# Aligned load buffers, a later place for flags and slot gates, and a new split of a gather over three engines

## The chip, the cores and the metric

The kernel runs on one core of a Trainium2 chip. The metric is the device time of one execution in microseconds (us): the median of several runs, and the span of one profiled execution, which is the time from its first to its last instruction in the profile.

## The reference

The reference first runs a gated recurrence over each of 4 sequences of 5056 steps with 256 channels, then sends every one of the 20,224 resulting rows to one of 8 experts. Each expert keeps at most the 80 rows with the highest gate weight; all other output rows are zero.

```python
sig = 1.0 / (1.0 + np.exp(-f_logit))
f = lower_bound + (1.0 - lower_bound) * sig
i = 1.0 - f
for t in range(S):                        # 4 sequences, 5056 steps, 256 channels
    h = f[:, t] * h + i[:, t] * x[:, t]
    y[:, t] = h
...
logits = y @ w_gate                       # 20224 rows, 8 experts
expert_idx = np.argmax(logits, axis=1)
gate_w = softmax(logits)[rows, expert_idx]
for e in range(8):
    tok_idx = rows of expert e, the 80 with the largest gate_w
    h = np.maximum(y[tok_idx] @ w1[e], 0.0)             # 256 -> 1024
    out[tok_idx] = gate_w[tok_idx, None] * (h @ w2[e])  # 1024 -> 256
```

All data are float32.

## The kernel before

The kernel has three stages on one core. The order of all instructions is written out by hand: within an engine the program order is the order of execution, and an instruction that waits holds up everything behind it on its engine.

**Loads and recurrence.** The work is cut into 40 units (10 groups of 512 steps by 4 sequences; the last group has 448). A unit loads a block of `f_logit` and a block of `x`, 512 KB each, through SyncE's DMA queue (SP) into the buffers `f_t` and `x_t` of the pool `ld`, four of each. Each partition gets four pieces of 1 KB per block. ScalarE (ACT) makes the sigmoid, GpSimd (POOL) multiplies it with `x`, TensorE (PE) transposes both into the channel layout, ACT and VectorE (DVE) finish the gate and run the scan, and the result stays in `h_all`, a buffer of all 20,224 columns. PE also computes the gate logits of each unit. From the ninth unit on SP also issues a clear of a 256 KB piece of the output for each unit, a copy from a zeroed DRAM buffer; `clear_rest` issues what is left in pieces of 1 MB after the last unit, behind the first six weight halves.

**Selection.** The largest gate weights of each expert are ranked, and the selected token numbers are put into `trow` (8 experts by 80 slots) on DVE, line 577; ACT copies slot gates and token numbers to `flat`, line 578. The function `settle` then does two things. `slots_down` transposes `flat` on PE and makes `gsl` (the gate weight of each slot, which `finish` uses) and `goal` (the output row of each slot, which `scatter` uses). After that DVE computes four flags per partition in `doubts`; they say whether the fast selection could be wrong. PE adds the flags up in `total`, line 687, and DVE turns them into `doubt` after expert 1. Only if `doubt` is above zero does a second, slower branch run.

**Experts.** For each expert e:

- `gather(e)` copies the 80 selected columns of `h_all` into `xe`. Three engines share the 80: each first loads its token numbers from `trow` into registers (line 618) and then copies column by column (line 622). DVE has 28 columns, ACT 28, POOL 24.
- `scaled(e)` on DVE multiplies `xe` into `xt`, in two instructions (line 629).
- `hidden(e)` on PE, 32 matmul passes (line 640), and `relu(e)` on ACT.
- `result(e)` on PE, 16 passes (line 655), and `finish(e)` on DVE, which scales by `gsl`.
- `scatter(e)` on POOL, an indirect DMA of 80 rows into the output.

Weights arrive in halves of 512 KB in the pool `wring`, seven buffers, issued by `more(1)` on SP as buffers come free. `wring` begins where `ld` began once the first stage has closed its pools. `busy(pool, m, tag)` issues m matmuls on PE whose result isn't used; it stands between stages, where PE would otherwise be without work.

The order around the change is `gather(0)`, `scaled(0)`, `settle()`, `busy(psl, 24, "rivals")`, `gather(1)`, `scaled(1)`, `hidden(0)`, `relu(0)`, `total`, `gather(2)`, `result(0)`, `scaled(2)`, `finish(0)`, `hidden(1)`, `relu(1)`; then a loop over e from 1 with `gather(e+2)`, `hidden(e+1)`, `relu(e+1)`, `result(e)`, `scaled(e+2)`, `finish(e)`, `scatter(e-1)`.

The pool `consts` holds the small tables, `trow`, `gsl`, `goal` and others; the `ld` pool follows it. In the built program the first load buffer begins at byte 25,568 of each partition, which is 480 past a multiple of 512, and since all load and weight buffers are 4 KB long and adjacent, each of them does. `h_all` is allocated from the other end of the memory.

Of the kernel before, what the change touches and what calls it, by code (L numbers as in the profile page):

```python
# [9 lines left out]
F32 = mybir.dt.float32  # L10
# [7 lines left out]
P = 128  # L18
# [5 lines left out]
def kernel(  # L24
# [11 lines left out]
    nc = tc.nc  # L36
# [10 lines left out]
    K = (capacity + TOP - 1) // TOP * TOP  # L47
# [22 lines left out]
    consts = ctx.enter_context(tc.tile_pool(name="consts", bufs=1))  # L70
# [31 lines left out]
    ones = consts.tile([P, 1], F32, name="ones")  # L102
# [25 lines left out]
    gsl = consts.tile([K, E], F32, name="gsl")  # L128
    goal = consts.tile([K, E], I32, name="goal")
    doubt = consts.tile([1, 1], I32, name="doubt")  # L130


    hpool = tc.alloc_tile_pool(name="hpool", bufs=1, side="right")
# [30 lines left out]
    def busy(pool, m, tag):  # L164
        warm = pool.tile([P, P], F32, name="warm", tag=tag)
        for _ in range(m):
            nc.tensor.matmul(warm, ident, ident, start=True, stop=True)  # L167
# [319 lines left out]
    def slots_down(flat, sp):  # L487

        nc.tensor.transpose(sp, flat, ident[:2 * E, :2 * E])
        nc.vector.tensor_copy(gsl, sp[:, ds(E, E)])  # L490
        far = consts.tile([K, E], F32, name="far", tag="far")
        nc.vector.tensor_scalar(out=far, in0=gsl, scalar1=0.0, scalar2=AWAY,
                                op0=ALU.is_le, op1=ALU.mult)
        nc.vector.tensor_tensor(goal, sp[:, :E], far, ALU.add)


    doubts = consts.tile([P, 6], F32, name="doubts")
    psl = ctx.enter_context(tc.tile_pool(name="psl", bufs=1, space=PSUM))
    with tc.tile_pool(name="sel", bufs=1) as sel:
# [15 lines left out]
        rivals = psl.tile([P, M + 3], F32, name="rivals", tag="rivals")  # L515
        sums_p = rivals[:, M:]
        rivals = rivals[:, :M]
        nc.tensor.matmul(rivals, mates, spread.rearrange("p c k -> p (c k)"),
                         start=True, stop=True)
# [51 lines left out]
        kept = psl.tile([P, K + 2 * E], F32, name="kept", tag="kept")  # L571
# [8 lines left out]
    def settle():  # L580


        low = consts.tile([P, DEEP], F32, name="low")
        d = doubts
        slots_down(flat, kept[:K, ds(K, 2 * E)])
        nc.vector.tensor_scalar(out=low, in0=taken, scalar1=-2.0, scalar2=2.0,
                                op0=ALU.mult, op1=ALU.add)
        nc.vector.tensor_tensor(low, low, vals, ALU.add)
        nc.vector.tensor_reduce(d[:, 4:5], low, AX.X, ALU.min)
        nc.vector.tensor_reduce(d[:, 5:6], tops[:, :, TOP - 1], AX.X, ALU.max)  # L590
        nc.vector.tensor_copy(d[:, 0:1], taken[:, DEEP - 1:])
        nc.vector.tensor_tensor(d[:, 1:2], d[:, 5:6], d[:, 4:5], ALU.is_ge)
        nc.vector.scalar_tensor_tensor(out=d[:, 2:3], in0=vals[:, ds(TOP - 1, 1)],
                                       scalar=vals[:, ds(TOP, 1)], in1=taken[:, ds(TOP, 1)],
                                       op0=ALU.is_le, op1=ALU.mult)
        nc.vector.tensor_scalar(d[:, 3:4], off[:, 2:3], float(capacity), off[:, 1:2],
                                ALU.min, ALU.not_equal)

    ways = [(mybir.EngineType.DVE, nc.vector.tensor_copy, 28),
            (mybir.EngineType.Activation, nc.scalar.copy, 28),  # L600
            (mybir.EngineType.Pool, nc.gpsimd.tensor_copy, K - 56)]
    ways = [w for w in ways if w[2] > 0]

    def experts(again):
        with tc.tile_pool(name="xp", bufs=2) as xp, \
             tc.tile_pool(name="mp", bufs=2) as mp, \
             tc.tile_pool(name="psh", bufs=4, space=PSUM) as psh, \
             tc.tile_pool(name="psy", bufs=2, space=PSUM) as psy:
            w = {} if again else w_sb
            late = list(order if again else order[3:])  # L610
            X, XT, HID, Y = {}, {}, {}, {}


            def gather(e):
                X[e] = xp.tile([P, DC, K], F32, name="xe", tag="xe")
                k = 0
                for engine, copy, n in ways:
                    _, at_tok = nc.values_load_multi_w_load_instructions(
                        trow[ds(e, 1), ds(k, n)], engines=(engine,), min_val=0, max_val=N - 1,
                        skip_runtime_bounds_check_because="token numbers come from iota")  # L620
                    for j, v in enumerate(at_tok):
                        copy(X[e][:, :, ds(k + j, 1)], h_all[:, :, ds(v, 1)])  # L622
                    k += n

            def scaled(e):
                XT[e] = mp.tile([P, DC, K], F32, name="xt", tag="xt")
                x_e = X.pop(e)
                for o in range(DC):
                    nc.vector.tensor_scalar_mul(XT[e][:, o], x_e[:, o], omlb[:, ds(o, 1)])  # L629

            def hidden(e):
                HID[e] = mp.tile([P, FC, K], F32, name="hid", tag="hid")
                xt = XT.pop(e)
                halves = w.pop((1, e))
                ps = []
                for i in range(2):
                    h_ps = psh.tile([P, CH, K], F32, name="h_ps", tag="h_ps")
                    for c in range(CH):
                        for o in range(DC):
                            nc.tensor.matmul(h_ps[:, c], halves[i][:, o, ds(c * P, P)], xt[:, o],  # L640
                                             start=o == 0, stop=o == DC - 1,
                                             skip_group_check=True)
                    ps.append(h_ps)
                return ps

            def relu(e, ps):
                for i in range(2):
                    nc.scalar.activation(HID[e][:, ds(i * CH, CH)], ps[i], ACT.Relu)  # L648

            def result(e):  # L650
                y_ps = psy.tile([K, D], F32, name="y_ps", tag="y_ps")
                halves = w.pop((2, e))
                hid = HID.pop(e)
                for c in range(FC):
                    nc.tensor.matmul(y_ps, hid[:, c], halves[c // CH][:, c % CH],  # L655
                                     start=c == 0, stop=c == FC - 1)
                return y_ps

            def finish(e, y_ps):
                Y[e] = mp.tile([K, D], F32, name="y", tag="y", bufs=3)  # L660
                nc.vector.tensor_scalar_mul(Y[e], y_ps, gsl[:, ds(e, 1)])  # L661

            def scatter(e):
                nc.gpsimd.indirect_dma_start(  # L664
                    out=out, out_offset=bass.IndirectOffsetOnAxis(ap=goal[:, ds(e, 1)], axis=0),
                    in_=Y.pop(e), in_offset=None, bounds_check=N - 1, oob_is_err=False)

            def more(m):
                for key in late[:m]:
                    w[key] = weights(*key)  # L670
                del late[:m]

            if again:
                more(3)
            gather(0)
            scaled(0)
            if not again:
                settle()
                busy(psl, 24, "rivals")
            gather(1)  # L680
            scaled(1)
            ps = hidden(0)
            relu(0, ps)
            more(1)
            if not again:
                total = psl.tile([1, 4], F32, name="total", tag="kept")
                nc.tensor.matmul(total, ones, doubts[:, :4], start=True, stop=True)
            gather(2)
            y_ps = result(0)
            more(1)  # L690
            scaled(2)
            finish(0, y_ps)
            ps = hidden(1)
            relu(1, ps)
            more(1)
            for e in range(1, E):
                if e + 2 < E:
                    gather(e + 2)
                if e + 1 < E:
                    ps = hidden(e + 1)  # L700
                    relu(e + 1, ps)
                    more(1)
                y_ps = result(e)
                more(1)
                if e + 2 < E:
                    scaled(e + 2)
                finish(e, y_ps)
                scatter(e - 1)
                if e == 1 and not again:
                    found = consts.tile([1, 1], F32, name="found")  # L710
                    nc.vector.tensor_reduce(found, total, AX.X, ALU.add)
                    nc.vector.tensor_copy(doubt, found)
            scatter(E - 1)

    experts(False)


# [83 lines left out]
```

## Time and profile before

| | |
|---|---|
| median of 3 runs | 256.51 us (255.76 to 257.93) |
| the profiled execution's own time | 258.45 us |
| its span in the profile | 256.3 us |
| busy PE, DVE, ACT, POOL | 213.3, 166.1, 138.2, 135.3 us |
| moved by DMA | 81.11 MB, mean 316 GB/s |
| mean granted clock of PE | 0.949 |

The page of the profile cuts the span into 40 equal columns of 6.4 us and gives for each column the busy share of each engine in tenths, the granted PE clock in tenths of full speed, the share of the 16 DMA engines and the rate. In lists of instructions a line has the start in us, the duration, the engine, the source line, the operation, what it writes and reads, and in brackets the idle time of the engine before it with what ended that idle time. PE shows two rows per matmul: the load of the weights (PEld) and the matmul; a float32 matmul is two passes, so `busy` with 24 shows 48.

### The profile page before, as it was taken

The numbers are of one execution on the slowest core, as the hardware profiler recorded it, in microseconds if no ns is written. First come the engines' busy times: TensorE is split into PE (matmuls) and PEld (weight loads), VectorE is DVE, ScalarE is ACT, GpSimd is POOL, SyncE is SP. The second block draws the span as 40 slices with busy tenths as digits, with TensorE's granted clock in tenths as the row PEclk, the third lists the DMA queues.
The fourth block names the chain that finished last, engine by engine and source line by source line (L and its number), as shares of the span: only waits on it lengthen the run. The fifth ranks groups of instructions, "written<-read, shape, count | busy, mean of one in ns | idle before, by whom it ended". The sixth has DMA issues, their size and how long they took to land.

```text
span 256.3 us, 6243 instructions
## 1 busy us (share of the span) xinstructions
PE 213.3 (83%) x1887; PEld 168.4 (66%) x1887; DVE 166.1 (65%) x466; ACT 138.2 (54%) x405; POOL 135.3 (53%) x273
## 2 busy tenths in 40 slices
PE   0669889998979799998879574986997999999990
PEld 0546667675757476766546462985887968888860
DVE  0997669695959499697749548575576706656210
ACT  1666668666678967766955443050455543445100
POOL 2758579577665769666566631011467156661111
PEclk9999999999999799999999978699999569999998
DMA  6999999999999999999999999999999968999700
GB/s 181 378 361 349 347 348 361 364 369 368 365 370 364 372 365 369 365 369 371 361 259 258 306 339 329 401 358 348 297 321 321 358 211 269 303 311 313 224 18 20
DMA packets 59386, 81.11 MB, mean 316 GB/s; under 512 B 3280, under 2 KB 52048, under 8 KB 56912
## 3 DMA queue, kind: packets, MB, share of 16 engines
q1 hardware_dynamic: 57888, 78.92, 94.3%
q10 hardware_dynamic: 1072, 1.06, 1.2%
q0 software_dynamic: 384, 0.66, 0.9%
q8 instruction: 17, 0.28, 0.4%
q14 instruction: 25, 0.20, 0.2%
HBM read 78.91 MB, written 22.41 MB: 395 GB/s over the span
## 4 chain that ended last, share of the span: by engine, by line
PE 33%; DMA 29%; issue 9%; ACT 9%; DVE 7%; SPq 6%; POOL 3%; DVEq 1%; POOLq 0%; ACTq 0%
DMA f_t<-in_f_logit_dram 14%; DMA x_t<-in_x_dram 9%; PE lg L262 7%; PE sp L233 6%; DMA out_dram<-y,goal 6%; PE up L233 6%; PE h_ps L640 5%; PE y_ps L655 3%; PE warm L167 3%; SPq L150 3%; ACT h_all L244 3%; ACT f_t L222 2%; DVE xe L622 2%; POOL x_t L226 2%; PE lt L277 1%
## 5 line engine op out<-in xcount | busy, mean ns | idle before, releaser
L226 POOL TENSOR_TENSOR x_t<-f_t,x_t 128x1024 f32<-128x1024 f32 (+1 forms) x40 | 95.0, 2378 | 49.2 <-DMA x_t<-in_x_dram 27.7
L250 DVE TENSOR_TENSOR_SCAN h_all<-h_all,up 128x512 f32<-128x512 f32 (+1 forms) x80 | 95.6, 1241 | 12.2 <-ACT h_all L244 10.9
L222 ACT ACTIVATE f_t<-f_t 128x1024 f32<-128x1024 f32 (+1 forms) x40 | 42.4, 1059 | 28.4 <-DMA f_t<-in_f_logit_dram 27.7
L233 PE MATMUL sp<-ident,f_t 128*128 128x128 f32 (+1 forms) x320 | 45.5, 286 | 10.3 <-ACT f_t L222 8.2
L244 ACT ACTIVATE h_all<-sp,nomlb 128x512 f32<-128x512 f32 (+1 forms) x80 | 50.0, 673 | 6.1 <-PE sp L233 5.8
L233 PEld LDWEIGHTS sp<-ident,f_t 128*128 128x128 f32 (+1 forms) x320 | 35.4, 145 | 27.0 <-issue 21.0
L233 PE MATMUL up<-ident,x_t 128*128 128x128 f32 (+1 forms) x320 | 44.2, 281 | 10.1 <-POOL x_t L226 7.4
L262 PE MATMUL lg<-h_all,wg 128*32 128x128 f32 (+1 forms) x640 | 43.5, 401 | 8.3 <-ACT ls L269 6.8
L233 PEld LDWEIGHTS up<-ident,x_t 128*128 128x128 f32 (+1 forms) x320 | 36.3, 145 | 14.1 <-POOL x_t L226 9.6
L622 DVE COPY xe<-h_all 128x2 f32 x224 | 26.5, 179 | 14.6 <-issue 14.6
L640 PEld LDWEIGHTS h_ps<-xt,w_sb 128*128 128x128 f32 x256 | 32.5, 207 | 3.0 <-DVE xt L629 1.9
L640 PE MATMUL h_ps<-xt,w_sb 128*128 128x80 f32 x256 | 32.7, 291 | 2.1 <-DVE xt L629 1.7
L262 PEld LDWEIGHTS lg<-h_all,wg 128*32 128x32 f32 x640 | 18.3, 120 | 21.3 <-ACT ls L269 8.7
L622 POOL COPY xe<-h_all 128x2 f32 x192 | 24.4, 203 | 14.4 <-issue 9.5
L655 PE MATMUL y_ps<-w_sb,hid 128*80 128x256 f32 x128 | 30.9, 399 | 0.0
L622 ACT COPY xe<-h_all 128x2 f32 x224 | 22.3, 190 | 13.2 <-issue 6.7
L655 PEld LDWEIGHTS y_ps<-w_sb,hid 128*80 128x80 f32 x128 | 19.8, 159 | 8.5 <-issue 1.5
L664 POOL DMA_INDIRECT out_dram<-y,goal x8 | 7.5, 939 | 30.8 <-DVE y L661 21.7
L167 PE MATMUL warm<-ident 128*128 128x128 f32 x140 | 18.7, 298 | 0.0
L167 PEld LDWEIGHTS warm<-ident 128*128 128x128 f32 x140 | 18.3, 214 | 0.0
L648 ACT ACTIVATE hid<-h_ps 128x320 f32<-128x320 f32 x16 | 7.0, 437 | 20.8 <-PE h_ps L640 20.8
L661 DVE TENSOR_SCALAR y<-y_ps,gsl 80x256 f32<-80x256 f32 x8 | 3.8, 479 | 19.2 <-PE y_ps L655 19.2
(110 smaller groups left out, 101.3 us busy)
## 6 DMA issues: line engine op xcount, KB each, us to landing
f_t<-in_f_logit_dram SPq DMA_DIRECT2D x36, 512.0 KB, 8.2
x_t<-in_x_dram SPq DMA_DIRECT2D x36, 512.0 KB, 9.0
w_sb<-in_moe_w_dram SPq DMA_DIRECT2D x32, 512.0 KB, 5.7
out_dram<-z_dram SPq DMA_DIRECT2D x40, 256.0 KB, 8.7
out_dram<-z_dram SPq DMA_DIRECT2D x9, 1024.0 KB, 19.8
f_t<-in_f_logit_dram SPq DMA_DIRECT2D x4, 448.0 KB, 11.4
x_t<-in_x_dram SPq DMA_DIRECT2D x4, 448.0 KB, 12.3
z_dram<-zero ACTq DMA_DIRECT2D x1, 1024.0 KB, 9.0
```

The lines of the kernel that those rows point to most:

```text
L150: nc.sync.dma_start(out=out_z[rows, ds(k * D, n)], in_=z_dram[rows, :n])
L167: nc.tensor.matmul(warm, ident, ident, start=True, stop=True)
L222: nc.scalar.activation(s_t, s_t, ACT.Sigmoid, scale=-1.0)
L226: nc.gpsimd.tensor_tensor(u_t, sts[n], u_t, ALU.mult)
L233: nc.tensor.transpose(ps[:, ds(r * k, k)], src[n][:, r, ds(o * P, P)], ident[:k, :k])
L244: nc.scalar.activation(columns(n, o), sps.pop((n, o)), ACT.Identity, scale=nomlb[:, ds(o, 1)], bias=1.0)
L250: nc.vector.tensor_tensor_scan(h, h, ups.pop((n, o)), h_all[:, o, ds(spot(n) - 1, 1)] if n >= B else 0.0, ALU.mult, ALU.add)
L262: nc.tensor.matmul(lgs[g][ds(r * LC, LC), b, :k], wg[:, o], columns(n, o)[:, r::R], start=o == 0, stop=o == DC - 1, skip_group_check=True)
L622: copy(X[e][:, :, ds(k + j, 1)], h_all[:, :, ds(v, 1)])
L640: nc.tensor.matmul(h_ps[:, c], halves[i][:, o, ds(c * P, P)], xt[:, o], start=o == 0, stop=o == DC - 1, skip_group_check=True)
L655: nc.tensor.matmul(y_ps, hid[:, c], halves[c // CH][:, c % CH], start=c == 0, stop=c == FC - 1)
L664: nc.gpsimd.indirect_dma_start(out=out, out_offset=bass.IndirectOffsetOnAxis(ap=goal[:, ds(e, 1)], axis=0), in_=Y.pop(e), in_offset=None, ...
```

## The change

Three things are altered.

- A tile `pad` of 8 floats (32 bytes per partition) is allocated at the end of the constants that stand ahead of the load buffers. It is never used. The load buffers, and later the weight buffers, begin 32 bytes later, at byte 25,600, a multiple of 512.
- The split of the gather's 80 columns goes from 28, 28, 24 to 25, 29, 26 for DVE, ACT and POOL.
- `settle()` moves from behind `scaled(0)` to behind `scaled(2)`, ahead of `finish(0)`. The sum of the flags, `total`, moves from behind `relu(0)` to behind `relu(1)`, ahead of the loop, and takes its buffer from the tag `rivals` instead of `kept`. `busy` behind `scaled(0)` has 22 matmuls instead of 24.

```diff
+    consts.tile([P, 8], F32, name="pad")
+
     hpool = tc.alloc_tile_pool(name="hpool", bufs=1, side="right")
...
-    ways = [(mybir.EngineType.DVE, nc.vector.tensor_copy, 28),
-            (mybir.EngineType.Activation, nc.scalar.copy, 28),
-            (mybir.EngineType.Pool, nc.gpsimd.tensor_copy, K - 56)]
+    ways = [(mybir.EngineType.DVE, nc.vector.tensor_copy, 25),
+            (mybir.EngineType.Activation, nc.scalar.copy, 29),
+            (mybir.EngineType.Pool, nc.gpsimd.tensor_copy, K - 54)]
...
             gather(0)
             scaled(0)
             if not again:
-                settle()
-                busy(psl, 24, "rivals")
+                busy(psl, 22, "rivals")
             gather(1)
             scaled(1)
             ps = hidden(0)
             relu(0, ps)
             more(1)
-            if not again:
-                total = psl.tile([1, 4], F32, name="total", tag="kept")
-                nc.tensor.matmul(total, ones, doubts[:, :4], start=True, stop=True)
             gather(2)
             y_ps = result(0)
             more(1)
             scaled(2)
+            if not again:
+                settle()
             finish(0, y_ps)
             ps = hidden(1)
             relu(1, ps)
             more(1)
+            if not again:
+                total = psl.tile([1, 4], F32, name="total", tag="rivals")
+                nc.tensor.matmul(total, ones, doubts[:, :4], start=True, stop=True)
             for e in range(1, E):
```

## The prediction

> **What bounds the kernel now.** I read the page first, its rows over time, then the timeline of the experts' stage engine by engine, then busy time by window around each drop of the clock, then the landings of the weights.
>
> ```profile
> PE   0669889998979799998879574986997999999990
> ...
> PEclk9999999999999799999999978699999569999998
> DMA  6999999999999999999999999999999968999700
> GB/s 181 378 361 349 347 348 361 364 369 368 365 370 364 372 365 369 365 369 371 361 259 258 306 339 329 401 358 348 297 321 321 358 211 269 303 311 313 224 18 20
> ```
>
> Each column is 6.4 us. The DMA row is full from the second column to the 32nd (about 205 us): until then bytes set the pace, first the 40 units of loads with clears between, then weights and the remaining clears. After that PE is full and DMA is not. The clock row has its deepest hole in columns 32 and 33, 198 to 211 us, exactly where the bound passes from DMA to PE.
>
> PE there, from the timeline:
>
> ```profile
> 193.65 3.69 PE L640 MATMUL h_ps<-xt,w_sb 128*128 128x80 f32 x32
> 199.06 6.77 PE L640 MATMUL h_ps<-xt,w_sb 128*128 128x80 f32 x32 [1.71 <-DVE xt L629]
> 205.62 5.64 PE L655 MATMUL y_ps<-w_sb,hid 128*80 128x256 f32 x16
> ...
> 218.09 3.70 PE L640 MATMUL h_ps<-xt,w_sb 128*128 128x80 f32 x32
> 221.62 3.62 PE L655 MATMUL y_ps<-w_sb,hid 128*80 128x256 f32 x16
> ```
>
> These are `hidden(1)`, `hidden(2)`, `result(1)`, and a later pair at full speed. Before `hidden(2)` PE stands still for 1.71 us, waiting for `xt` of expert 2; then the same 32 matmuls take 6.77 instead of 3.69 us and the next 16 take 5.64 instead of 3.62. `hidden(3)` begins at 211.10; from there the pair repeats every 6.99 us without a hole until 249.65, so whatever is gained before 211 is gained at the end.
>
> Busy time by window (length, PE, PEld, DVE, ACT, POOL, granted clock, DMA share, GB/s), cut at the clock's own steps, which are 3.41 us apart:
>
> ```profile
> 83.42:86.83 3.41, 1.79 (x20) 0.89 (x12) 2.15 (x3) 3.41 (x5) 2.29 (x1) 1.00 1.07 369
> 114.14:117.55 3.41, 2.18 (x27) 1.37 (x26) 3.41 (x5) 2.55 (x5) 2.38 (x1) 1.00 1.08 370
> 172.17:175.58 3.41, 1.69 (x16) 1.50 (x14) 2.16 (x11) 1.01 (x4) 1.83 (x7) 1.00 1.01 346
> 196.06:199.47 3.41, 1.70 (x16) 1.55 (x15) 3.00 (x23) 0.56 (x3) 2.29 (x19) 1.00 1.06 377
> 199.47:202.89 3.42, 3.42 (x19) 3.42 (x17) 2.13 (x19) 3.10 (x29) 0.00 (x0) 0.50 1.08 373
> ```
>
> The windows at 83.42 and 196.06 had PE busy 52% and 50%, and the next window ran at 0.50. At 114.14 it was 64% and the clock stayed. At 172.17 it was 50% and stayed too, so 50% is the edge; no window of 62% or more was followed by a drop. The drop at 199.47 lasted three windows, 10.24 us.
>
> **What feeds the hole.** VectorE, from the timeline:
>
> ```profile
> 185.95 0.43 DVE L629 TENSOR_SCALAR xt<-xe,omlb 128x80 f32<-128x80 f32 x2
> ...
> 187.65 0.21 DVE L596 TENSOR_SCALAR doubts<-off 128x1 f32<-128x1 f32 x1
> 189.49 3.29 DVE L622 COPY xe<-h_all 128x2 f32 x28 [1.63 <-issue]
> 192.92 0.43 DVE L629 TENSOR_SCALAR xt<-xe,omlb 128x80 f32<-128x80 f32 x2
> ...
> 198.74 0.43 DVE L629 TENSOR_SCALAR xt<-xe,omlb 128x80 f32<-128x80 f32 x2
> ```
>
> Between two scalings lie a load of token numbers (1.63) and 28 copies (3.29, 0.1175 each); after the first scaling `settle` comes as well, from 186.38 to 187.86, 1.48 us. VectorE is the last of the three gathering engines in the first three gathers.
>
> The weights of `hidden(2)` are nearly as late, from the issues of that tile:
>
> ```profile
> L453 SPq DMA_DIRECT2D w_sb<-in_moe_w_dram x1: 374/374/374, 175.8 to 175.8; - x1
> ...
> DMA to landing us min/median/max: 22.7/22.7/22.7
> ```
>
> Issued at 175.78 behind ten clears, the first half lands at 198.52; the second (issued 188.3, 11.6 to landing) at 199.91. DMA is full all that time, so these times stay unless bytes move faster.
>
> **The change, part by part.**
>
> *Fewer columns on VectorE* (28 to 25; ACT 29, POOL 26). Three copies of 0.1175 are 0.35 us per gather; the load of numbers (1.86 us for 28 columns on VectorE, 1.56 for 24 on POOL, so some 0.065 a column) may give 0.2 more; bounds 0.35 and 0.55, I take 0.45. POOL's copies take 0.127: two more and their numbers are 0.4 us, from an end at 185.09 to 185.5 in the first gather, level with VectorE's (185.83 less 0.45). `xt` of expert 0 comes some 0.4 earlier, 185.55, and PE begins `hidden(0)` at about 185.9 instead of 186.31. In the second and third gathers POOL would end near 190.3 and 195.0, VectorE at 190.4 and 195.7: still VectorE. ACT's one more (0.1 and 0.06) ends first. Later in the loop POOL ended gather 6 at 223.87 while `hidden(6)` began at 225.07, room enough for 0.4.
>
> *`settle` behind `scaled(2)`.* The second scaling loses 1.48 and 2 x 0.45 and ends at about 190.95; the third at about 196.25 instead of 199.17. `settle` runs then, to about 197.75. Behind it on VectorE wait `finish(0)` (199.09 before, 197.8 now: still earlier) and the load for gather 3, whose `xt` would be ready near 203.2. Nobody downstream loses: the first scatter went at 204.18.
>
> *The added wait.* `total` now stands on PE between `hidden(1)` and `hidden(2)` and needs the last flag of `settle`: 197.75 and a little, plus its own 0.19, so PE is free of it at 198.05. Behind it in PE's order stands `hidden(2)`, and behind that ACT's `relu(2)` and `result(1)`. It costs nothing because the weights (198.52) are later still; without that cover it would cost PE what `settle` ends after 197.4.
>
> *PE before it.* The transpose of `flat` (0.21) goes from ahead of the warm-up to ahead of `hidden(1)`. The warm-up needn't wait for ACT's copy: it begins at 179.6 instead of 180.30, and 44 passes of 0.117 end at 184.8 instead of 185.92. PE then idles 1.1 us before `hidden(0)`; a window that holds all of it is 68% busy, on the safe side. `hidden(0)` ends 189.7, `result(0)` begins when ACT has the first half, about 190.0 (190.13), and with the transpose `hidden(1)` ends at about 197.4, as before (197.34).
>
> So the hole before `hidden(2)` goes from 1.71 us to 198.55 - 197.4 = 1.15, of which `total` fills 0.19: a window of at least 66%. By the rows above the clock stays up. `hidden(2)` from 198.55 takes 3.69 (its second half needs the weights of 199.91 at 200.4), `result(1)` 3.62, and `hidden(3)` begins at 205.86 instead of 211.10: **-5.2 us**, of which 0.5 is the earlier start and 4.7 the clock. The weights that follow (204.37, 205.74, 207.19, 208.64) land before they are used on this schedule too, and `xt(3)` at 203.2 as well. SP's issues keep their order; neither moved piece holds a DMA.
>
> *The 32 bytes.* Load and weight buffers begin at 0 instead of 480 past a multiple of 512. No row shows a load into the new place. In the trace's DMA records the least time of a 1 KB packet into these buffers is 46 ns, of 2 KB into them 84, of the 8 KB packets from DRAM to DRAM, which touch no buffer here, 309. All lie on 8.4 ns plus 37.6 per KB. If the offset cost anything, the loads should lie above the line of the clears. Hence I take nothing. The far end of a gain: with 1 KB at the clears' 309/8 = 38.6 ns the loads would stop setting the pace and PE would. From 60 to 120 us, 367 GB/s are 16.8 units of 1.31 MB, 3.57 us each, of which PE was busy 54.8/16.8 = 3.26; over the 31 units with clears that is 9.6 us at most. The far end of a loss: PE-bound stages can't lose, and the loads alone ran at 348 GB/s where 46 ns allow 356, so a like step down, 2% of some 120 us of loading, is 2.5 us. Ends -9.6 and +2.5.
>
> The Trainium skill, "DMA: Bandwidth & Descriptors", section "How a descriptor splits into AXI transactions", says a descriptor that starts off a 256-byte boundary fetches from the boundary below and pays for those bytes; a 1 KB piece 224 past one would be 39 beats instead of 32. By that estimate an aligned load takes 18% less time, and the sum would go to the PE limit, 241.7. The scatters' packets, read from such buffers, speak against it: one row took 46 ns, four rows 159, again 37.7 a row.
>
> The skill's page "TensorE: Matmul & The Clock Gate", section "What's actually happening", has the half clock come after an idle window of about 3.4 us. By it a hole of 1.71 us would not have cost anything and nothing but 0.5 us could be won; the rows of 196.06 and 199.47 contradict it.
>
> Sum against the profiled execution: its span 256.3 becomes 251.1, its time 258.45 (2.15 lie around the span) becomes 253.2. The median of the runs shown is 1.94 below the profiled time; 256.51 - 5.2 = **251.3**.
>
> **The rivals.**
>
> *The clock falls all the same.* If the windows fall otherwise, or the weights land 0.5 us later, the hole is again near half a window. For: 1.15 us is not zero, and the landing sits behind 200 us of full queues. Against: all windows of 62% or more. Only the earlier start stays: 256.0.
>
> *Aligned buffers load faster.* For: that part is done for nothing else. Against: the line of packet times. Full price 251.3 - 9.6 = 241.7; partial, up to 249.
>
> *The sum of the flags becomes the stop.* If the gathers don't shorten, because POOL with 26 columns is the last, `settle` ends after 199.06 and `total` holds `hidden(2)` longer than `xt` did. It decides from 1.3 us above my 197.75. A start at 199.7 costs 0.6 against before; PE then stands 2.3 us, the clock falls, and one more window at half clock costs 1.7: 256.5 + 2.3 = 258.8.
>
> **How the numbers follow.** Clock held 0.50, its own range 249 to 253.6 (half the clock's 4.7 either way); clock falls anyway 0.22; faster loads 0.14; flags' sum 0.14. A measurement here can tell about 1%, 2.6 us. Faster 0.64 (the first and third), the same 0.22, slower 0.14. The range 243 to 258 leaves out about half of each outer case.
>
> **What would show it.** Right: granted clock 1.00 in every window from 196 to 250; `hidden(2)` near 198.5 and 3.7 us long; `hidden(3)` near 205.9; `total` just ahead of `hidden(2)`; 1 KB packets at 46 ns and loads at 348 GB/s. Wrong: a half clock at 199, or a hole ahead of `hidden(0)` over 1.6 us; loads-only columns above 360 GB/s; a PE wait for VectorE's flags.

## The result and the profile after

The changed kernel takes 267.44 us (266.34 to 269.81), the kernel before on the same chip 256.98: a ratio of 1.042, 95% interval 1.034 to 1.051. It is 4.2% slower. The profiled execution has a span of 265.0 us, 8.7 more than before.

The page over time, columns of 6.6 us:

```profile
PE   0789999999996899897898696929779849969990
...
PEclk9999999999999999999999689995599995995998
DMA  7999999999999999999998999999377873894410
GB/s 186 381 385 383 385 386 391 390 393 388 393 390 391 391 391 390 394 387 333 316 383 302 399 397 344 314 326 276 109 224 232 267 245 97 253 303 139 141 31 20
```

Two opposite things happened. In the load stage, from the second to the 18th column, the rate is 381 to 394 GB/s where it was 347 to 378, and DMA is full for a shorter time. In the experts' stage, from the 26th column on, the clock row has three holes instead of one, DMA is no longer full, and PE has gaps.

VectorE marks both. The first line writes the token table, the others begin the scalings of experts 0, 1 and 2:

```profile
168.70 0.23 DVE L580 CAST trow<-kept 8x80 int32<-8x80 f32 x1 [2.00 <-PE kept L577]
...
178.62 0.43 DVE L632 TENSOR_SCALAR xt<-xe,omlb 128x80 f32<-128x80 f32 x2 [4.09 <-POOL xe L625]
...
187.62 0.43 DVE L632 TENSOR_SCALAR xt<-xe,omlb 128x80 f32<-128x80 f32 x2 [4.04 <-POOL xe L625]
...
196.76 0.43 DVE L632 TENSOR_SCALAR xt<-xe,omlb 128x80 f32<-128x80 f32 x2 [4.14 <-ACT xe L625]
```

In the kernel before the first of these lines is

```profile
179.63 0.23 DVE L577 CAST trow<-kept 8x80 int32<-8x80 f32 x1 [2.00 <-PE kept L574]
```

The table is written at 168.70 now and was at 179.63 before. That is 10.9 us won. The scalings then lie 9 us apart instead of 6 to 7, and VectorE, which used to be the last of the three gathering engines, stands 4 us and waits for POOL or ACT. From the table to the end of the last `result` it was 179.63 to 249.65, 70.0 us; now it is 168.70 to 258.57, 89.9 us: 19.9 lost. 19.9 - 10.9 = 9.0, of the span's 8.7; the rest lies behind the last `result`.

What POOL and ACT do in those 4 us is in the list of the line that loads token numbers into registers (duration in ns, least, median, most). The changed kernel:

```profile
L621 POOLq TENSOR_LOAD <-trow x8: 5799/6022/6298, 169.0 to 237.3; - x8
L621 DVEq TENSOR_LOAD <-trow x8: 1845/1850/2103, 169.0 to 237.3; - x8
L621 ACTq TENSOR_LOAD <-trow x8: 6159/6426/6695, 169.0 to 235.4; - x8
```

The kernel before:

```profile
L618 POOLq TENSOR_LOAD <-trow x8: 1538/1559/1772, 179.9 to 225.8; - x8
L618 DVEq TENSOR_LOAD <-trow x8: 1850/1858/2118, 179.9 to 232.3; - x8
L618 ACTq TENSOR_LOAD <-trow x8: 1730/1737/1951, 179.9 to 228.8; - x8
```

26 numbers instead of 24 cost POOL 6.0 us instead of 1.6, 29 instead of 28 cost ACT 6.4 instead of 1.7; VectorE's 25 cost what its 28 did, 1.85. PE, in the same execution, runs into it before expert 0:

```profile
178.99 7.08 PE L643 MATMUL h_ps<-xt,w_sb 128*128 128x80 f32 x32 [5.22 <-issue]
187.91 5.48 PE L658 MATMUL y_ps<-w_sb,hid 128*80 128x256 f32 x16 [1.84 <-ACT hid L651]
...
198.82 0.19 PE L699 MATMUL total<-doubts,ones 128*1 128x4 f32 x2 [1.56 <-DVE doubts L599]
198.94 3.79 PE L643 MATMUL h_ps<-xt,w_sb 128*128 128x80 f32 x32
```

PE stands 5.22 us before `hidden(0)`, the clock falls, and `hidden(0)` and `result(0)` run at half speed. `hidden(2)`, where the clock fell before, does run at full speed (3.79 us), behind a wait for the flags' sum.

### The profile page after: what moved, and what is told of

Read it like the earlier page. It is cut to its first block, busy times and chain, and to the rows that moved or that the text cites. A ratio compares the mean times of both kernels' runs of the same rounds, so it can differ in the third digit from the quotient of the medians.

```text
span 265.0 us, 6235 instructions
## 1 busy us (share of the span) xinstructions
PE 218.3 (82%) x1883; PEld 172.8 (65%) x1883; DVE 162.5 (61%) x442; ACT 137.6 (52%) x413; POOL 136.9 (52%) x289
## 3 DMA queue, kind: packets, MB, share of 16 engines
q1 hardware_dynamic: 57888, 78.92, 86.8%
## 4 chain that ended last, share of the span: by engine, by line
PE 52%; issue 12%; ACT 11%; DVE 7%; DMA 7%; POOL 4%; ACTq 3%; SPq 1%; DVEq 1%; POOLq 0%
PE y_ps L658 11%; PE h_ps L643 10%; PE lg L265 10%; PE sp L236 9%; PE up L236 7%; DMA x_t<-in_x_dram 4%; ACT h_all L247 3%; DVE h_all L253 3%; POOL x_t L229 3%; PE warm L170 3%; DMA f_t<-in_f_logit_dram 3%; ACT xe L625 3%; ACTq L621 3%; PE lt L280 2%; ACT ls L272 1%
## 5 line engine op out<-in xcount | busy, mean ns | idle before, releaser
L625 POOL COPY xe<-h_all 128x2 f32 x208 | 26.2, 202 | 49.4 <-issue 31.9
L625 ACT COPY xe<-h_all 128x2 f32 x232 | 23.2, 194 | 48.5 <-issue 29.9
L643 PE MATMUL h_ps<-xt,w_sb 128*128 128x80 f32 x256 | 37.5, 317 | 11.9 <-issue 10.8
L236 PE MATMUL up<-ident,x_t 128*128 128x128 f32 (+1 forms) x320 | 43.2, 277 | 4.4 <-POOL x_t L229 2.9
L643 PEld LDWEIGHTS h_ps<-xt,w_sb 128*128 128x128 f32 x256 | 36.5, 230 | 13.5 <-issue 11.8
L658 PE MATMUL y_ps<-w_sb,hid 128*80 128x256 f32 x128 | 33.3, 421 | 1.8 <-ACT hid L651 1.8
L625 DVE COPY xe<-h_all 128x2 f32 x200 | 23.5, 170 | 13.8 <-issue 13.8
L658 PEld LDWEIGHTS y_ps<-w_sb,hid 128*80 128x80 f32 x128 | 21.1, 170 | 11.6 <-issue 3.1
L632 DVE TENSOR_SCALAR xt<-xe,omlb 128x80 f32<-128x80 f32 x16 | 3.5, 258 | 33.2 <-POOL xe L625 25.3
L305 ACT COPY shift<-lt 128x128 f32<-128x128 f32 (+1 forms) x10 | 2.7, 267 | 16.5 <-DVE lt L304 16.5
## 6 DMA issues: line engine op xcount, KB each, us to landing
out_dram<-z_dram SPq DMA_DIRECT2D x40, 256.0 KB, 6.9
```

The source lines that it names most:

```text
L236: nc.tensor.transpose(ps[:, ds(r * k, k)], src[n][:, r, ds(o * P, P)], ident[:k, :k])
```

## The experiments

### Each part by itself

The first four kernels take the change apart. My theory: the aligned buffers make the loads faster, and the split makes the loads of token numbers slow. The rival: the new order costs the time.

The 32 bytes alone:

```diff
+    consts.tile([P, 8], F32, name="pad")
```

> The kernel before with the 32 bytes alone; split 28, 28, 24 and the old order stay. Theory (aligned buffers load faster; the loss comes from the new split): loads alone run at 384 GB/s or more instead of 348, the selection begins some 10.6 us earlier as in the changed kernel, nothing is lost behind it: median near 246.5 us (256.5 less 10). Rival (the faster loads came from something else in the change, or are given back by a later wait): median within 2 us of 256.5, or the selection earlier and the end not.

Measured: 247.52 us against 256.01, ratio 0.963 (0.956 to 0.970). The token table is written at 169.08. Nothing is given back later: from there to the end of the last `result` it is 70.0 us, as before. The 10.6 us between 179.63 and 169.08 are more than the 8.5 of the medians. Some 2 us of them need not be the buffers': in the profiled execution of the kernel before PE's clock was at half for 3.4 us from 86.8 us on. The profile of the order alone, with the buffers in their old place, has no such fall between 60 and 120 us, and its table is written at 177.68, 8.6 after 169.08. The rate of the loads alone, before the first clear, in the windows (length, five engines' busy time, clock, DMA share, GB/s); the kernel before:

```profile
20.00:34.00 14.00, 12.28 (x129) 8.47 (x128) 10.15 (x9) 9.93 (x14) 10.07 (x5) 1.00 1.09 348
```

and with the 32 bytes:

```profile
20.00:34.00 14.00, 13.28 (x141) 10.00 (x142) 10.62 (x9) 10.89 (x16) 11.04 (x6) 1.00 1.09 384
```

The split alone:

```diff
-    ways = [(mybir.EngineType.DVE, nc.vector.tensor_copy, 28),
-            (mybir.EngineType.Activation, nc.scalar.copy, 28),
-            (mybir.EngineType.Pool, nc.gpsimd.tensor_copy, K - 56)]
+    ways = [(mybir.EngineType.DVE, nc.vector.tensor_copy, 25),
+            (mybir.EngineType.Activation, nc.scalar.copy, 29),
+            (mybir.EngineType.Pool, nc.gpsimd.tensor_copy, K - 54)]
```

> The kernel before with the split 25, 29, 26 alone. Theory (ACT's and POOL's loads of token numbers, which now begin 100 and 216 bytes into a row of the table, take 6.4 and 6.0 us instead of 1.7 and 1.6): both durations as in the changed kernel, an expert's gather some 4 us longer, and a median near 276 us (the changed kernel needs 90 us from the token table to the last scatter, the one before 71). Rival (the loads are slow because of the new order, in which something else holds the table or the queue): loads near 1.7 us and a median within 2 us of 256.5.

Measured: 278.16 us, ratio 1.083 (1.076 to 1.091). ACT's load takes 6.39 us and POOL's 5.96 in the median, and table to last `result` is 89.95 us, as in the changed kernel. The split causes the whole loss of 19.9 us behind the table; the rival falls. The medians differ by 2.3 us more. In this profile the table is written at 179.96, 2.3 later than in that of the order alone, behind a half clock from 176.4 to 179.8; why the clock fell there stays open.

The order alone, which is the last three parts of the change's diff (`settle`, `busy`, `total`):

```diff
-                settle()
-                busy(psl, 24, "rivals")
+                busy(psl, 22, "rivals")
...
             scaled(2)
+            if not again:
+                settle()
...
+                total = psl.tile([1, 4], F32, name="total", tag="rivals")
```

> The kernel before with settle, the sum of the flags and the warm-up of 22 moved as in the change, split 28, 28, 24, no 32 bytes. My prediction's mechanism: settle's 1.48 us leave the path to the third scaling, but the weights of hidden(2) land at 198.5 all the same; the hole before hidden(2) shrinks from 1.7 us to some 1.2 and the clock stays up: median 251 to 252. Rival (the sum of the flags stops PE as long as the scaling did): the hole stays over 1.6 us, the clock falls, median 256 to 258.

Measured: 257.34 us, ratio 1.004 (0.9998 to 1.008). My expectation missed and the rival's held; no clear gain or loss, since the interval includes 1. PE in this run:

```profile
191.65 3.80 PE L642 MATMUL h_ps<-xt,w_sb 128*128 128x80 f32 x32
197.43 0.19 PE L698 MATMUL total<-doubts,ones 128*1 128x4 f32 x2 [1.99 <-DVE doubts L598]
197.56 7.08 PE L642 MATMUL h_ps<-xt,w_sb 128*128 128x80 f32 x32
```

`settle` left the path to the third scaling, but the flags' sum ahead of `hidden(2)` waits for the same `settle` behind that scaling. The hole is 1.99 us against 1.71 and the clock falls as before.

All but the split:

```diff
-    ways = [(mybir.EngineType.DVE, nc.vector.tensor_copy, 25), ...
+    ways = [(mybir.EngineType.DVE, nc.vector.tensor_copy, 28), ...
```

> The changed kernel with the split put back to 28, 28, 24. Theory (the split alone costs the time): loads of token numbers back at 1.6 to 1.9 us, the selection as early as in the changed kernel, median near 243 us, far below both kernels. Rival (the new order costs the time): median above 257 us still.

Measured: 248.70 us, ratio 0.967 (0.959 to 0.974); loads of token numbers 1.57 to 1.86 us. So the split's price holds here too (267.44 less 248.7 is 18.7). My 243 missed by 5.7: I had again counted on the clock, and it fell (`hidden(2)` 7.01 us behind a hole of 1.98), as with the order alone:

```profile
189.26 0.19 PE L699 MATMUL total<-doubts,ones 128*1 128x4 f32 x2 [1.98 <-DVE doubts L599]
189.39 7.01 PE L643 MATMUL h_ps<-xt,w_sb 128*128 128x80 f32 x32
```

### What makes a load of token numbers slow

ACT's and POOL's loads differ from VectorE's in three ways: the engine, the count, and the first slot. A split by expert separates them.

```diff
-                for engine, copy, n in ways:
+                d, a, p = (w[:2] for w in ways)
+                for (engine, copy), n in plans[e](d, a, p):
```

> The changed kernel with another split for each expert, to time the load of token numbers by engine, first slot and count. Experts 0 to 5 in the order VectorE, ACT, POOL: 28 28 24, 27 28 25, 26 28 26, 25 28 27, 24 28 28, 28 25 27; expert 6 in the order ACT 30, POOL 24, VectorE 26; expert 7 POOL 25, ACT 27, VectorE 28. Theory (the first slot decides: a load that begins off a multiple of 4 slots, 16 bytes, reads word by word at some 0.22 us a column): slow, 5.5 to 6.3 us, where the first slot is 27, 55, 26, 54, 25, 53, 30, 25; fast, 1.6 to 1.9, where it is 0, 28, 56, 24, 52, whatever the count and the engine; VectorE slow too when it starts at 54 (expert 6). Rival (the count decides: not a multiple of 4): slow for counts 27, 25, 26, 30 even from slot 0, fast for 28 from slot 27. Second rival (ACT and POOL alone have it): VectorE fast in expert 6.

Measured: 259.30 us in one run, of use only for the loads. Their durations in the trace, as first slot, count, us:

| expert | first engine | second | third |
|---|---|---|---|
| 0 | DVE 0, 28: 2.10 | ACT 28, 28: 1.94 | POOL 56, 24: 1.77 |
| 1 | DVE 0, 27: 2.33 | ACT 27, 28: 5.94 | POOL 55, 25: 5.59 |
| 2 | DVE 0, 26: 2.08 | ACT 26, 28: 5.97 | POOL 54, 26: 5.85 |
| 3 | DVE 0, 25: 1.85 | ACT 25, 28: 6.00 | POOL 53, 27: 6.02 |
| 4 | DVE 0, 24: 1.61 | ACT 24, 28: 1.74 | POOL 52, 28: 1.82 |
| 5 | DVE 0, 28: 1.85 | ACT 28, 25: 1.77 | POOL 53, 27: 6.28 |
| 6 | ACT 0, 30: 2.20 | POOL 30, 24: 5.59 | DVE 54, 26: 6.06 |
| 7 | POOL 0, 25: 1.82 | ACT 25, 27: 6.06 | DVE 52, 28: 1.87 |

(Expert 0's loads include some 0.2 us that every first load here has.) The first slot decides, on each of the three engines: a load of 28 on ACT takes 1.74 us from slot 24 and 5.94 from slot 27. A start on a multiple of four slots is a multiple of 16 bytes; a start 8 bytes off one, slots 26, 54 and 30, is as slow as one 4 off. Off it, each number costs 0.21 to 0.23 us (28 in 5.94, 24 in 5.59). On it, four together cost about that (VectorE: 24 in 1.61, 28 in 1.85), and each number left over costs as much as a group of four (25 in 1.85, 26 in 2.08, 27 in 2.33). The count thus plays a small part, up to 0.7 us; both rivals fall.

The Trainium skill, "Runtime: NRT & Kernel Launch", section "Instruction fetch mechanics", gives some 200 ns a register for this instruction even in bulk, speaking of register loads that the runtime adds. The slow loads here, from a table on the chip, come near it (0.21 to 0.23); the aligned ones need that time for four numbers.

The change as it stands, with only the starts put right: ACT loads 30 numbers from slot 24 and drops one, POOL 28 from slot 52 and drops two.

```diff
-                        trow[ds(e, 1), ds(k, n)], engines=(engine,), min_val=0, max_val=N - 1,
+                        trow[ds(e, 1), ds(k - k % 4, n + k % 4)], engines=(engine,), min_val=0, max_val=N - 1,
...
-                    for j, v in enumerate(at_tok):
+                    for j, v in enumerate(at_tok[k % 4:]):
```

> The changed kernel, split 25, 29, 26 kept, but ACT loads 30 numbers from slot 24 and drops the first, POOL 28 from slot 52 and drops two, so every load begins on a multiple of 16 bytes. Theory (start of the load): loads of 1.6 to 2.0 us and a median near 246 to 248 us, 20 below the changed kernel; the three columns fewer on VectorE are then worth up to 2 us against split 28, 28, 24 with the same order (248.7). Rival (count): still some 6 us a load and a median near 267 us.

Measured: 241.48 us, ratio 0.944 (0.940 to 0.948), 26 us below the changed kernel and 6 to 7 below what I expected: loads of 2.19 (ACT) and 1.82 (POOL), and this time the clock holds until the last `result`. PE:

```profile
182.90 3.80 PE L643 MATMUL h_ps<-xt,w_sb 128*128 128x80 f32 x32
186.62 0.19 PE L699 MATMUL total<-doubts,ones 128*1 128x4 f32 x2
186.75 3.80 PE L643 MATMUL h_ps<-xt,w_sb 128*128 128x80 f32 x32
190.38 3.62 PE L658 MATMUL y_ps<-w_sb,hid 128*80 128x256 f32 x16
```

`hidden(2)` follows `hidden(1)` with no hole. With VectorE's 28 columns the new order gained nothing (257.34, and 248.70 with the 32 bytes); with 25 and even starts the same order gives 241.48. The shorter share in the old order, with even starts, was not run, so how much of these 7.2 us needs the new order is not shown.

### The boundary for the load buffers

Three other places for the same buffers.

```diff
+    consts.tile([P, 24], F32, name="pad")     # 64 past a multiple of 512
+    consts.tile([P, 40], F32, name="pad")     # 128 past
+    consts.tile([P, 72], F32, name="pad")     # 256 past
```

> The kernel before with a tile of 96 bytes ahead of the load buffers: they begin 64 past a multiple of 512. Theory A (64 bytes are enough, since before they lay 32 off a multiple of 64): loads alone at 384 GB/s or more, 0.9 of the 1 KB packets at 46 ns, time near 247.5. Theory B (only larger boundaries count): loads at 348 GB/s, time near 256.

> The kernel before with a tile of 160 bytes: load buffers begin 128 past a multiple of 512. At 64 past the loads alone ran at 348 GB/s, at 256 past and at 0 at 384. If 256 is the boundary that counts: 348 and a time near 255. If 128 is enough: 384 and near 247.

> The kernel before with a tile of 288 bytes ahead of the load buffers: they begin 256 past a multiple of 512. If 256 or less is the boundary that counts: loads alone at 384 GB/s or more and a time near 247.5. If it is 512: loads at 348 to 367 GB/s and a time near 256.

| first load buffer, past a multiple of 512 | loads alone, 20 to 34 us | loads and clears, 60 to 120 us | time, us |
|---|---|---|---|
| 480 (before) | 348 GB/s | 367 GB/s | 256.0 (median) |
| 64 | 348 | 375 | 254.65 (one run) |
| 128 | 349 | 387 | 251.64 (one run) |
| 256 | 384 | 390 | 247.01 (one run) |
| 0 | 384 | 390 | 247.52 (median) |

(The kernel before that ran beside 128 had 256.99 us, the others 256.0.) Of the five places the two on a multiple of 256 have the full rate; 512 isn't needed. For loads alone the other three cost the same: at 16 engines, 1 KB takes 47.1 ns (16 KB at 348 GB/s) instead of 42.7. With clears between, 64 and 128 lie in between; why, these runs do not tell.

By the rule of the skill's DMA page that my prediction weighed, a 1 KB piece has 7 beats more for an offset of 224, 2 for one of 64 and 4 for one of 128. The page states it for the bytes that are fetched; here the offset is on the side that is written. The boundary of 256 and the direction agree with it; its differences by offset are not in the loads alone, and the gain is 10% in rate, not 22.

### The clock, and the steps of the prediction by themselves

If the half clock behind the hole costs the time and not the wait, work that is of no use but fills the hole must win it back. This kernel is the one with the 32 bytes alone, in the old order:

```diff
+            if not again:
+                busy(psl, 6, "rivals")
             for e in range(1, E):
```

> The kernel before with the 32 bytes, and 6 matmuls of the identity whose result is not used put on PE between hidden(1) and hidden(2), some 1.4 us of work into the hole of 1.7. Theory (the half clock behind the hole is what costs, not the wait): the clock stays at 1.00, hidden(2) takes 3.7 us instead of 6.9 and result(1) 3.6 instead of 5.5, median near 242.7 (247.5 less 4.8). Rival (the clock falls whatever PE does there, or another wait takes over): median within 1.5 us of 247.5.

Measured: 241.47 us, ratio 0.943 (0.935 to 0.950), 6.0 below the same kernel without the six matmuls. PE without them, in the run of the 32 bytes alone:

```profile
188.51 6.91 PE L642 MATMUL h_ps<-xt,w_sb 128*128 128x80 f32 x32 [1.72 <-DVE xt L631]
195.22 5.49 PE L657 MATMUL y_ps<-w_sb,hid 128*80 128x256 f32 x16
```

and with them:

```profile
185.50 1.54 PE L169 MATMUL warm<-ident 128*128 128x128 f32 x12
187.35 3.80 PE L642 MATMUL h_ps<-xt,w_sb 128*128 128x80 f32 x32 [0.31 <-DVE xt L631]
190.99 3.62 PE L657 MATMUL y_ps<-w_sb,hid 128*80 128x256 f32 x16
```

`xt` ends the wait here as before, but the clock stays up. From the table to the end of the last `result` it is 65.1 us instead of 70.0; the 4.9 are what `hidden(2)` and `result(1)` won, and the rest of the 6.0 lies ahead of the table, where the six matmuls change nothing. This is shown, then: the hole's price is the clock.

Then the case that my prediction worked out: the change with even starts and without the 32 bytes.

```diff
-    consts.tile([P, 8], F32, name="pad")
...
+                        trow[ds(e, 1), ds(k - k % 4, n + k % 4)], ...
```

> The changed kernel without its 32 bytes and with the loads of token numbers on multiples of four slots: what is left is what my prediction worked out with nothing for the 32 bytes. If its steps for the split, for settle and for the clock hold: the clock stays up after 196 us, hidden(2) starts near 198.5 and takes 3.7 us, median 251 to 252. Rival (without the faster loads the weights of hidden(2) land too late and the clock falls): median 255 to 257.

Measured: 251.81 us, ratio 0.982 (0.974 to 0.990), so 1.0 to 2.6% faster.

```profile
197.51 3.77 PE L642 MATMUL h_ps<-xt,w_sb 128*128 128x80 f32 x32 [0.72 <-DMA w_sb<-in_moe_w_dram]
201.11 3.62 PE L657 MATMUL y_ps<-w_sb,hid 128*80 128x256 f32 x16
```

`hidden(2)` waits 0.7 us for its weights, then runs at full speed.

A split with all starts and counts on multiples of four:

```diff
+    ways = [(mybir.EngineType.DVE, nc.vector.tensor_copy, 24),
+            (mybir.EngineType.Activation, nc.scalar.copy, 32),
+            (mybir.EngineType.Pool, nc.gpsimd.tensor_copy, K - 56)]
```

> The changed kernel with the split 24, 32, 24: all starts and counts multiples of four. By the loads timed so far (0.23 us for each four numbers, 0.2 fixed) VectorE's load takes 1.61 us, ACT's 1.95, POOL's 1.56, and VectorE has one copy fewer than with 25. Theory: clock held, loads of those lengths, median 240.5 to 241.5, as fast as 25, 29, 26 with even starts or up to 1 us faster. Rival (ACT with 32 copies becomes the last of each gather): 242 to 244.

Measured: 242.54 us, ratio 0.945 (0.938 to 0.953): loads of 1.61, 1.97 and 1.56 us, clock held. The interval overlaps that of 25, 29, 26 with even starts, so no difference between the two is shown.

## Why the prediction was wrong, step by step

**The step that turned the sign: "the load of numbers (1.86 us for 28 columns on VectorE, 1.56 for 24 on POOL, so some 0.065 a column)".** I had two durations, both of loads that begin on a multiple of 16 bytes, drew a line through them, across two engines, and used it for loads that begin at 100 and 216 bytes. I priced POOL's two extra columns with their numbers at 0.4 us a gather and ACT's one at 0.16; the loads alone grew by 4.5 and 4.7. What the line promised VectorE did not come either: its 25 numbers took 1.85 us, as its 28 did, because each number beyond a group of four costs as much as a group. In medians the split costs 22.2 us by itself (278.16 less 256.01; 19.9 of it behind the token table) and 18.7 inside the change. I gave this step bounds of 0.35 and 0.55 for VectorE and none at all for a start that no row of the trace shows. The new start of the two other shares was the unknown operation of this change, and I didn't see it as one.

**The second: "The 32 bytes. ... Hence I take nothing."** Measured: 8.5 us in the medians; the profile's 10.9 hold some 2 us that need not be the buffers'. The far end that I wrote down, 9.6, was near the right size. What misled me is the least record. It is 46 ns for 1 KB before and after, but in the loads alone of the kernel before (20 to 34 us) only 41% of the 1 KB records took 46 ns, and their mean was 49.8; with the 32 bytes nearly all took 46 (mean 46.05). The line through the least times hid this, though the trace before had it. And 46 ns is no ceiling: I let it allow 356 GB/s, and the loads ran at 384. The records add up to 1.09 of the engines' time in both kernels, so they overlap; a share over 1 stood in the rows that I quoted.

**The mechanism that I forecast held where it could.** With the split's loads put right and without the 32 bytes, 251.81 us stand against a forecast of 251.3: the clock stays up, `hidden(2)` starts at 197.5 (forecast 198.5), waits for its weights and takes 3.77 (3.69). Counted from the token table, the third scaling ends at 16.7 us (forecast 16.6) and `settle` at 18.15 (18.12). The 0.5 us of earlier start did not come: `hidden(2)` starts 19.6 behind the table, against 18.9 forecast and 19.4 before, since its weights set it; that it lies within 1 us of 198.5 in the profile is luck, as the table came 1.75 earlier in this execution. From the table to the end of the last `result` it is 65.2 us instead of 70.0, so the 4.7 of the clock came. That PE loses the clock, not the wait, is shown by the kernel with the hole filled.

**Of the rivals, two came true in part.** "Aligned buffers load faster" was right. "The sum of the flags becomes the stop" is what the order does when VectorE keeps its 28 columns (a hole of 1.99 us, 257.34); in the changed kernel `hidden(2)` waits for it too, 1.56 us, but there the clock holds and the time is lost in the gathers. I had the share of POOL becoming the last as its cause, and POOL's and ACT's did become the last, for a reason ten times as large as the one I priced.

The parts: -8.5 for the 32 bytes, +1.3 for the order (its interval includes no change), +18.7 for the split on top of them, together +11.5; measured +10.5 against the before of its own comparison. The 18.7 is itself the distance of the changed kernel from the one with both other parts, so the sum tests only that these two add; with the 22.2 of the split by itself it would be 15.0.

## What to carry to other kernels

A change of a few columns can move the start of something else, so list every address that a change moves, and take a start that the trace has not shown as an unknown with a price on both sides. Read the cost of a transfer from the rate of a stage in which nothing but it runs, not from the least of its records. Where PE's clock falls behind a short hole, a few matmuls without use in the hole can win the clock back although the wait stays: here some 5 us.

## What the runs showed of the hardware

- Loads of numbers from on-chip memory into an engine's registers took some 0.23 us for each four where the first lay on a multiple of 16 bytes, and 0.21 to 0.23 us for each one where it lay 4, 8 or 12 bytes past one (ACT and POOL at all three, VectorE at 8, run by_expert).
- Loads in 1 KB pieces ran at 384 GB/s into buffers at 0 and 256 bytes past a multiple of 512, and at 348 to 349 at 64, 128 and 480 past a multiple of 512.
- A hole of 1.7 to 2.0 us before `hidden(2)` was followed by the half clock for 10.2 us in the four profiles that had it in that place (before, the 32 bytes alone, the order alone, all but the split); in the 3.41 us step of the clock ahead of the fall PE was busy 42% to 50%. With 0.3 or 0.7 us, or none, the clock stayed, and also with 1.56 us in the changed kernel and 1.66 in the split by expert (no step there under 66%), and with 1.99 us before `hidden(7)` in the split alone, where the hole lay across two steps (70% and 72%). The share of one step does not settle it: before `hidden(3)` of the split alone a hole of 2.91 us lay across two, 51% and 63%, and the half clock followed the second.
